# Key-value products in column groups and score products in quarters, in a float32 linear-attention and SoLU kernel

## The chip, the cores and the metric

The kernel runs on one core of a Trainium2 chip. The metric is the device time of one execution in microseconds (us). Before the change, nine runs have a median of 420.47 us and lie between 418.76 and 420.90.

TensorE multiplies matrices: a load (LDWEIGHTS) puts the stationary operand into the array, and a matmul then streams the moving operand through it. Results land in PSUM[...]. VectorE (DVE), ScalarE (ACT) and GpSimd (POOL) do the rest, each with its own queue of instructions; SyncE (SP) issues transfers.

## The reference

A recurrent attention runs over 4 batches, 8 heads, 768 tokens and a head size of 48. Its output, viewed as 3072 tokens by 384, goes through a feed-forward block with a softmax-weighted activation and a layer norm.

```python
for t in range(S):
    cur = np.einsum('bhd,bhe->bhde', u[None] * kt, vt)
    y[:, :, t] = np.einsum('bhd,bhde->bhe', rt, state + cur)
    state = w[None, :, :, None] * state + np.einsum('bhd,bhe->bhde', kt, vt)
...
h = x @ w_in
sm = e / (np.sum(e, axis=-1, keepdims=True) + 1e-09)    # e = exp(h - max)
solu = h * sm
ln = (solu - mu) / np.sqrt(var + 1e-06) * g_ln
return ln @ w_out
```

Everything is float32; w_in is 384 by 1024 and w_out is 1024 by 384.

## The kernel before

The kernel has a direct path, which runs here, and a general path behind a flag, which doesn't run. All that follows is in the direct path.

**Tiling.** The tokens are cut into 24 units of 128: six chunks (index c, C = 6) for each of four batches, with the batches innermost. A unit needs the state that the unit four places before it left, which belongs to the same batch. Heads are handled in four pairs (HP = 4, index a): the two heads of a pair (index q) lie at partitions 0 to 47 and 64 to 111 of a tile, with zeros between (P = 64 partitions for each head, of which D = 48 are used).

**Order.** The schedule is written out by hand: the loop at L829 issues the steps, and each engine takes its instructions in that order. One turn i holds, in TensorE's order:

- turn_r and turn_k of unit i + 2: transposes of r (tr_ps, L698) and of the decayed k (tk_ps, L706)
- turn_ln of unit i - 7: transposes of the activation (t_ps, L806)
- ffn_in of unit i - 2: the product with w_in (h_ps, L775), 12 records
- scores of unit i + 1: k times r per head (at, L717)
- ffn_out of unit i - 7: the product with w_out (o_ps, L817), 16 records
- finish of unit i: r times the state and scores times v (y_ps, L745), then k times v (kv_ps, L761)

Steps of units that don't exist yet, or any more, are left out. During the first turns the weights also arrive by DMA, are turned from 8-byte into float32 numbers by ScalarE, VectorE and GpSimd (L510 to L541), and column sums are taken of w_out (mean_ps, L653).

A float32 matmul appears in the trace as two records, each with a load; a transpose appears as one.

**Scores.** For each pair a and each head q, one matmul takes kT (48 rows, 128 columns) as the stationary and rT (48 rows, 128 columns) as the moving operand. The result, 128 tokens by 128 tokens, goes to the bank of q (at0 or at1, from pool psA with two buffers). Then VectorE copies it with a mask into AT (L720), only where the second token is later than the first.

**State.** After y_ps, finish computes k times v for a pair at once: kp of both heads (128 columns) is stationary, and v of both heads (96 columns) moves. Half of the result is the product of one head's k with the other head's v, and isn't wanted. The tile wt holds w^128 in the wanted blocks and zeros in the others. VectorE adds the product to the state (L764), and GpSimd multiplies the sum by wt (L765), which also sets the unwanted blocks back to zero. In the first chunk, VectorE does both at once (L767). The step is absent in the last chunk, so 20 units have it.

make_wt (L605) fills wt on GpSimd, in turn -1. The states aren't set to zero beforehand.

**Start.** VectorE first clears the pads of kpads and rpads (L482, L483), then waits for w to be turned by TensorE (wd_ps, L572), and builds the tables of powers of w (tab, pw; L573 to L583). TensorE turns one of them (kd_ps, L590), ScalarE copies it out (kdec, L591), and with kdec GpSimd decays k (kp, L675). GpSimd also makes ident, the identity for transposes, and the mask later.

**Banks.** PSUM has eight banks: two for at, two for h_ps, and four (pool psM, tag m) which tr_ps, tk_ps, t_ps, o_ps, y_ps, kv_ps and the means use in turn.

Of the kernel before, what the change touches and what calls it, by code (L numbers as in the profile page):

```python
# [9 lines left out]
F32 = mybir.dt.float32  # L10
U32 = mybir.dt.uint32
ACT = mybir.ActivationFunctionType
ALU = mybir.AluOpType
AX = mybir.AxisListType
PSUM = bass.MemoryType.PSUM
# [381 lines left out]
def direct_path(  # L397
# [26 lines left out]
    nc = tc.nc  # L424
    B, H, S, D = r.shape
    T = 128
    P = 64
    C = S // T
    HP = H // 2
    dm = H * D  # L430
# [10 lines left out]
    const = ctx.enter_context(tc.tile_pool(name="const", bufs=1))  # L441
# [1 line left out]
    fpool = ctx.enter_context(tc.tile_pool(name="fpool", bufs=2))  # L443
    wpool = ctx.enter_context(tc.tile_pool(name="wpool", bufs=2))
    small = ctx.enter_context(tc.tile_pool(name="small", bufs=4))
    psA = ctx.enter_context(tc.tile_pool(name="psA", bufs=2, space=PSUM))
    psH = ctx.enter_context(tc.tile_pool(name="psH", bufs=1, space=PSUM))
    psM = ctx.enter_context(tc.tile_pool(name="psM", bufs=4, space=PSUM))

# [12 lines left out]
    def load(i, which="krv"):  # L462
        b, c = units[i]
        for t, src, n in ((kpads, k, "k"), (rpads, r, "r"), (vts, v, "v")):
            if n in which:
                nc.sync.dma_start(out=t[i % len(t)][:, :, 0:D],
                                  in_=src[b, :, ts(c, T), :].rearrange("h s d -> s h d"))
# [12 lines left out]
                        in_=u.rearrange("h d -> (h d)").partition_broadcast(128))  # L480
    for i in range(NLD):
        nc.vector.memset(kpads[i][:, :, D:P], 0.0)  # L482
        nc.vector.memset(rpads[i][:, :, D:P], 0.0)  # L483

    def words(x):
        n, m = x.shape
        t = bass.DRamTensorHandle(x.tensor.name, (n, 2 * m), U32)
        return bass.AP(tensor=t, offset=0, ap=[[2 * m, n], [1, 2 * m]])
# [69 lines left out]
    ident = const.tile([128, 128], F32, name="ident")  # L558
# [4 lines left out]
    nc.gpsimd.memset(neg_half, -0.5)  # L563

    tab = const.tile([128, 2, HP, T], F32, name="tab")
    back, fore = tab[:, 0], tab[:, 1]
    pw = const.tile([128, 2, 8, HP], F32, name="pw")
# [27 lines left out]
    nc.gpsimd.affine_select(out=mf, in_=mf, compare_op=ALU.is_gt, fill=0.0, base=0,  # L597
                            pattern=[[1, T]], channel_multiplier=-1)
    nc.gpsimd.tensor_copy(out=later[:, 0, :], in_=mf)


    states = [const.tile([128, HP, 2, D], F32, name=f"state{b}") for b in range(B)]
    wt = const.tile([128, HP, 2, D], F32, name="wt")

    def make_wt():  # L605

        nc.gpsimd.memset(wt, 0.0)
        for q in range(2):
            rows = slice(q * P, q * P + D)
            nc.gpsimd.tensor_copy(out=wt[rows, :, q, :],  # L610
                                  in_=pw[rows, 0, 7].unsqueeze(2).to_broadcast([D, HP, D]))

    N = len(units)
    sums = const.tile([128, N], F32, name="sums")
# [53 lines left out]
    def pair(t, a):  # L668
        return t[:, 2 * a : 2 * a + 2, :].rearrange("p q d -> p (q d)")
# [9 lines left out]
    def weigh(i, engine):  # L679
        rku = live[i]["rku"] = apool.tile([128, H, D], F32, name="rku")  # L680
        engine.tensor_mul(rku, kpads[i % NLD][:, :, 0:D], u_bc)
        engine.tensor_mul(rku, rku, rpads[i % NLD][:, :, 0:D])  # L682

    def sum_own(i):
        own = live[i]["own"] = small.tile([128, H, 1], F32, name="own")
        nc.vector.tensor_reduce(out=own[:, :, 0], in_=live[i]["rku"], axis=AX.X, op=ALU.add)
# [7 lines left out]
    def turn_r(i):  # L694
        rT = live[i]["rT"] = apool.tile([128, HP, T], F32, name="rT", bufs=3)
        ps = psM.tile([128, HP, T], F32, tag="m", name="tr_ps")
        for a in range(HP):
            nc.tensor.transpose(ps[:, a, :], pair(rpads[i % NLD], a), ident)  # L698
        nc.vector.tensor_mul(rT, ps, fore)

    def turn_k(i):
        X = live[i]
        X["kT"] = apool.tile([128, HP, T], F32, name="kT")
        ps = psM.tile([128, HP, T], F32, tag="m", name="tk_ps")
        for a in range(HP):
            nc.tensor.transpose(ps[:, a, :], pair(X["kp"], a), ident)  # L706
        nc.scalar.copy(out=X["kT"], in_=ps)


    def scores(i):  # L710
        X = live[i]
        A4 = X["AT"].rearrange("p (a q) t -> p a q t", q=2)
        pss = [psA.tile([128, HP, T], F32, tag="at", name=f"at{q}") for q in range(2)]
        for a in range(HP):
            for q in range(2):
                rows = slice(q * P, q * P + D)
                nc.tensor.matmul(pss[q][:, a, :], X["kT"][rows, a, :], X["rT"][rows, a, :],  # L717
                                 start=True, stop=True)
        for q in range(2):
            nc.vector.copy_predicated(A4[:, :, q, :], later.to_broadcast([128, HP, T]), pss[q])  # L720

# [12 lines left out]
    def finish(i):  # L734
        b, c = units[i]
        X = live[i]
        vt, AT, St = vts[i % NV], X["AT"], states[b]
        vf = vt.rearrange("p h d -> p (h d)")
        y_ps = psM.tile([128, KD, 128], F32, tag="m", name="y_ps")
        last = {m: n for n, (m, h, at) in enumerate(inner)}  # L740
        opened = set()

        def into(m, lhsT, rhs, stop):
            j, g = divmod(m, 4)
            nc.tensor.matmul(y_ps[32 * g : 32 * g + 32, j, :], lhsT, rhs, start=(g not in opened),  # L745
                             stop=stop, skip_group_check=True)
            opened.add(g)

        if c > 0:
            for m in range(12):  # L750
                a, n = divmod(m, 3)
                into(m, St[:, a].rearrange("p q d -> p (q d)")[:, ts(n, 32)], X["rT"][:, a, :],
                     False)
        for n, (m, h, at) in enumerate(inner):
            into(m, vf[:, at : at + 32], AT[:, h, :], last[m] == n)
        X["xT"] = fpool.tile([128, KD, 128], F32, name="xT", bufs=LA + 1)
        nc.scalar.copy(out=X["xT"], in_=y_ps)
        if c < C - 1:
            kv_ps = psM.tile([128, HP, 2, D], F32, tag="m", name="kv_ps")
            for a in range(HP):  # L760
                nc.tensor.matmul(kv_ps[:, a], pair(X["kp"], a), vt[:, 2 * a : 2 * a + 2, 0:D],  # L761
                                 start=True, stop=True)
            if c > 0:
                nc.vector.tensor_add(St, kv_ps, St)  # L764
                nc.gpsimd.tensor_mul(St, St, wt)  # L765
            else:
                nc.vector.tensor_mul(St, kv_ps, wt)  # L767


    def ffn_in(i):  # L770
# [58 lines left out]
    for i in range(-2, N + LA + LO):  # L829
        j, l = i - LA, i - LA - LO  # L830
        if i == 0:
            nc.sync.dma_start(out=g_sb, in_=moe_g_ln.rearrange("(c p) -> p c", p=128))
        if 0 <= i and i + 4 < N:
            load(i + 4)
        if i + 2 < N:
            turn_r(i + 2)
            if i == -2:
                weigh(0, nc.vector)
            sum_own(i + 2)
            turn_k(i + 2)  # L840
        fs = [pieces[p][2] for p in now if pieces[p][2] is not None]
        for p in now:
            convert_d(p)
        now = [todo.pop(0) for _ in range(conversions.get(i, 0))]
        for n, p in enumerate(now):
            convert_a(p)
            if n == 0 or i < LA:
                convert_b(p)
            if ahead < len(pieces):
                load_weights(ahead)  # L850
                ahead += 1
        if i + 3 < N:
            decay_k(i + 3)
            if i < 0:
                weigh(i + 3, nc.gpsimd)
        for p in now[: 1 if i >= LA else 2]:
            convert_c(p)
        if 0 <= i and i + 3 < N:
            weigh(i + 3, nc.gpsimd)
        if i == -1:  # L860
            make_wt()
        if i == 10:
            check_range()
        if 0 <= l and not i > N + LA - 1:
            turn_ln(l)
        if 0 <= j < N:
            ffn_in(j)
        column_sums(fs)
        if 0 <= i + 1 < N:
            scores(i + 1)  # L870
        if 0 <= j < N:
            unit(j)
        if i + 2 < N and (i < 0 or l >= 0):
            diagonal(i + 2)
        if i >= N + LA - 1 and l + 1 < N:
            turn_ln(l + 1)
        if l == N - 1:
            check_sums()
        if 0 <= l:
            ffn_out(l)  # L880
        if 0 <= i < N:
            finish(i)
        if l < 0 <= i:
            diagonal(i + 2)
        for p in now[1:] if i >= LA else []:
            convert_b(p)
            convert_c(p)
        if KF - 1 in fs:
            column_mean()
            for f in range(KF):  # L890
                centre(f, nc.vector if f % 2 == 0 else nc.gpsimd)
# [43 lines left out]
```

## Time and profile before

| What | Value |
|---|---|
| Median of nine runs | 420.47 us (418.76 to 420.90) |
| The profiled execution | 420.26 us |
| Its span, from the first to the last instruction | 418.5 us |
| Granted TensorE clock, mean | 0.981 |
| TensorE busy with matmuls | 393.8 us (94%) |
| TensorE busy with loads (beside matmuls) | 247.3 us (59%) |
| VectorE, ScalarE, GpSimd busy | 155.6, 181.1, 147.9 us (37%, 43%, 35%) |
| at, L717: 384 records | 30.1 us busy |
| kv_ps, L761: 160 records | 23.5 us busy |
| VectorE's addition to the state, L764: 16 | 8.9 us, 558 ns each |
| GpSimd's product with wt, L765: 16 | 16.1 us, 1005 ns each |
| GpSimd's filling of wt, L607 and L610 | 0.4 and 0.9 us |

The profile is of one execution. A record of a matmul runs from its dispatch to a modelled end, so records overlap, and the time that a stage takes is read from the distance between starts, or from the chain of waits, better than from the length of records. A line of the timeline has the start, the length, the engine, the line of the kernel, the operation, the tile written and the tiles read, the shape, and how many instructions were merged into it. Its length runs from the first start to the last end.

### The profile page before, as it was taken

To read this page: it belongs to the slowest core of one execution; us is meant where nothing else is said; L and a number is where in the kernel's file an instruction comes from. 1 tells how busy PE (TensorE), PEld (TensorE's weight loads), DVE (VectorE), ACT (ScalarE), POOL (GpSimd) and SP (SyncE) were. 2 spreads that over 40 slices of the span, in tenths; PEclk is the share of its full clock that TensorE was granted. 3 is DMA by queue.
4 is the path that set the end of the run, shared out by engine and by line. 5 is a ranking of instruction groups with operands and counts; after the bars stand their busy time and mean duration, and the time that the engine had idled before them with its cause. 6 is when DMAs were issued, how large, how long until landed. Compare 5 with 4: busy or idle time off the path is not lost.

```text
span 418.5 us, 7217 instructions
## 1 busy us (share of the span) xinstructions
PE 393.8 (94%) x2873; PEld 247.3 (59%) x2873; DVE 155.6 (37%) x302; ACT 181.1 (43%) x424; POOL 147.9 (35%) x220
## 2 busy tenths in 40 slices
PE   2699899979999999999999999999999999999994
PEld 1485455655665666656656656756755655556662
DVE  5988666546224243223322422422331322022110
ACT  1875787662452552542543533523524522223210
POOL 4886666847414514414324334234130110011000
PEclk9869999999999999999999999999999999999999
DMA  8999694100403403404304214124000000000101
GB/s 172 281 198 251 138 171 76 20 2 0 77 20 58 77 2 75 77 2 75 73 3 77 59 18 77 34 42 77 20 0 20 21 1 20 20 20 19 38 19 48
DMA packets 81593, 25.93 MB, mean 62 GB/s; under 512 B 76557, under 2 KB 79758, under 8 KB 81550
## 3 DMA queue, kind: packets, MB, share of 16 engines
q1 hardware_dynamic: 81406, 25.18, 29.8%
q8 instruction: 24, 0.39, 0.4%
q10 hardware_dynamic: 144, 0.20, 0.1%
q14 instruction: 19, 0.16, 0.1%
HBM read 20.65 MB, written 4.72 MB: 61 GB/s over the span
## 4 chain that ended last, share of the span: by engine, by line
PE 84%; DVE 7%; ACT 4%; POOL 1%; issue 1%; DMA 1%; ACTq 0%; POOLq 0%; DVEq 0%
PE o_ps L817 30%; PE h_ps L775 29%; PE y_ps L745 7%; PE at L717 5%; PE t_ps L806 5%; PE kv_ps L761 3%; PE tk_ps L706 2%; DVE AT L720 2%; ACT AT L692 2%; DVE solu L787 2%; PE tr_ps L698 1%; DVE ma L524 1%; DVE ma L526 1%; DVE mag L520 1%; PE mean_ps L653 1%
## 5 line engine op out<-in xcount | busy, mean ns | idle before, releaser
L775 PE MATMUL h_ps<-w_in_sb,xT 128*128 128x512 f32 x288 | 129.0, 597 | 2.5 <-DVE solu L787 2.1
L817 PE MATMUL o_ps<-w_out_sb,lnT 128*128 128x384 f32 x384 | 129.5, 491 | 0.0
L817 PEld LDWEIGHTS o_ps<-w_out_sb,lnT 128*128 128x128 f32 x384 | 71.2, 190 | 47.5 <-issue 1.0
L775 PEld LDWEIGHTS h_ps<-w_in_sb,xT 128*128 128x128 f32 x288 | 53.3, 192 | 61.1 <-issue 59.8
L720 DVE COPY_PREDICATED AT<-later,at 128x512 f32<-128x512 uint32 x48 | 32.2, 724 | 93.2 <-ACT e L778 82.9
L778 ACT ACTIVATE e<-h_ps 128x1024 f32<-128x1024 f32 x24 | 24.5, 1022 | 91.3 <-PE h_ps L775 91.3
L692 ACT ACTIVATE AT<-ident,own 128x128 f32<-128x128 f32 x192 | 58.5, 389 | 0.0
L791 POOL TENSOR_TENSOR st<-st 128x1 f32<-128x1 f32 x24 | 4.7, 198 | 140.1 <-DVE solu L787 140.1
L789 ACT ACTIVATE e<-solu 128x1024 f32<-128x1024 f32 x24 | 25.4, 1057 | 66.5 <-DVE solu L787 66.5
L717 PEld LDWEIGHTS at<-rT,kT 48*128 48x128 f32 x384 | 25.2, 195 | 18.0 <-issue 15.0
L764 DVE TENSOR_TENSOR state<-kv_ps,state 128x384 f32<-128x384 f32 x16 | 8.9, 558 | 69.2 <-PE kv_ps L761 69.2
L675 POOL TENSOR_TENSOR kp<-kpad,kdec 128x512 f32<-128x512 f32 x24 | 31.9, 1329 | 5.3 <-ACT kdec L591 5.2
L765 POOL TENSOR_TENSOR state<-state,wt 128x384 f32<-128x384 f32 x16 | 16.1, 1005 | 47.5 <-DVE state L764 47.5
L717 PE MATMUL at<-rT,kT 48*128 48x128 f32 x384 | 30.1, 293 | 1.4 <-ACT mag L510 1.3
L787 DVE SCALAR_TENSOR_TENSOR solu<-h_ps,st,e 128x1024 f32<-128x1024 f32 x24 | 30.8, 1284 | 1.1
L808 DVE COPY lnT<-t_ps 128x512 f32<-128x512 f32 x24 | 16.4, 683 | 36.5 <-PE t_ps L806 36.5
L806 PE MATMUL t_ps<-ident,solu 128*128 128x128 f32 x192 | 25.8, 277 | 2.3 <-ACT mean_sb L661 2.1
L745 PE MATMUL y_ps<-AT,vt 128*32 128x128 f32 x768 | 26.3, 279 | 0.0
L820 ACT ACTIVATE o<-o_ps,st 128x384 f32<-128x384 f32 x24 | 13.6, 568 | 29.1 <-PE o_ps L817 14.0
L806 PEld LDWEIGHTS t_ps<-ident,solu 128*128 128x128 f32 x192 | 22.0, 142 | 5.5 <-ACT mean_sb L661 2.3
L682 POOL TENSOR_TENSOR rku<-rku,rpad 128x384 f32<-128x384 f32 x23 | 23.4, 1015 | 1.8
L761 PE MATMUL kv_ps<-vt,kp 128*128 128x96 f32 x160 | 23.5, 292 | 0.0
(80 smaller groups left out, 362.6 us busy)
## 6 DMA issues: line engine op xcount, KB each, us to landing
kpad<-in_k_dram SPq DMA_DIRECT2D x24, 192.0 KB, 4.0
rpad<-in_r_dram SPq DMA_DIRECT2D x24, 192.0 KB, 4.0
vt<-in_v_dram SPq DMA_DIRECT2D x24, 192.0 KB, 4.2
out_dram<-o SPq DMA_DIRECT2D x24, 192.0 KB, 2.1
raw<-in_moe_w_in_dram SPq DMA_DIRECT2D x6, 512.0 KB, 5.6
raw<-in_moe_w_out_dram SPq DMA_DIRECT2D x8, 384.0 KB, 3.9
u_bc<-in_u_dram ACTq DMA_DIRECT2D x1, 192.0 KB, 3.4
wq<-in_w_dram SPq DMA_DIRECT2D x1, 1.5 KB
```

The lines of the kernel that those rows point to most:

```text
L675: nc.gpsimd.tensor_mul(X["kp"].rearrange("p h d -> p (h d)"), kpads[i % NLD].rearrange("p h d -> p (h d)"), kdec.rearrange("p a d -> p (a ...
L692: nc.scalar.activation(out=AT[:, h, :], in_=ident, func=ACT.Copy, scale=X["own"][:, h])
L717: nc.tensor.matmul(pss[q][:, a, :], X["kT"][rows, a, :], X["rT"][rows, a, :], start=True, stop=True)
L720: nc.vector.copy_predicated(A4[:, :, q, :], later.to_broadcast([128, HP, T]), pss[q])
L745: nc.tensor.matmul(y_ps[32 * g : 32 * g + 32, j, :], lhsT, rhs, start=(g not in opened), stop=stop, skip_group_check=True)
L761: nc.tensor.matmul(kv_ps[:, a], pair(X["kp"], a), vt[:, 2 * a : 2 * a + 2, 0:D], start=True, stop=True)
L775: nc.tensor.matmul(h_ps[:, ts(n, NX)], X["xT"][:, j, :], w_in_sb[:, j, ts(n, NX)], start=(j == 0), stop=(j == KD - 1))
L778: nc.scalar.activation(out=e, in_=h_ps, func=ACT.Exp, accum_out=sums[:, i : i + 1])
L787: nc.vector.scalar_tensor_tensor(out=solu, in0=X["h"], scalar=rs, in1=X["e"], op0=ALU.mult, op1=ALU.mult, accum_out=tot)
L789: nc.scalar.activation(out=X["e"], in_=solu, func=ACT.Square, accum_out=ss)
L806: nc.tensor.transpose(t_ps[:, f, :], X["solu"][:, ts(4 * g + f, 128)], ident)
L817: nc.tensor.matmul(o_ps, X["lnT"][:, f, :], w_out_sb[:, f, :], start=(f == 0), stop=(f == KF - 1))
```

## The change

- **scores**: the 128 columns of kT are taken in two groups of 64 (index c). The first group multiplies all 128 columns of rT. The second multiplies only the last 64, since a later token can't lie before it. One matmul per pair and head becomes two, and the two groups write to different halves of the partitions of a bank. A quarter of each bank is never written.
- **Score banks**: at0 and at1 are made once, at the top, and VectorE sets them to zero there, ahead of the tables.
- **k times v**: one matmul per head instead of one per pair, with 64 stationary and 48 moving columns. The two heads of a pair go to partitions 0 to 63 and 64 to 127 of kv_ps, which is now 4 by 48 wide. The products of one head's k with the other's v are no longer computed.
- **State update**: two additions on VectorE and two products on GpSimd, each on 64 partitions by 4 by 48 elements, for the wanted blocks only. The factor is read from pw, repeated along the last axis.
- **wt and make_wt** are removed. ScalarE sets the four states to zero (an activation with scale 0 on a column of ident), ahead of kdec.

```diff
-    psA = ctx.enter_context(tc.tile_pool(name="psA", bufs=2, space=PSUM))
+    psA = ctx.enter_context(tc.tile_pool(name="psA", bufs=1, space=PSUM))
...
+    pss = [psA.tile([128, HP, T], F32, name=f"at{q}") for q in range(2)]
+    for ps in pss:
+        nc.vector.memset(ps, 0.0)
...
+    states = [const.tile([128, HP, 2, D], F32, name=f"state{b}") for b in range(B)]
+    for St in states:
+        nc.scalar.activation(out=St.rearrange("p a q d -> p (a q d)"),
+                             in_=ident[:, 0:1].to_broadcast([128, dm]), func=ACT.Copy, scale=0.0)
...
-    wt = const.tile([128, HP, 2, D], F32, name="wt")
-    def make_wt():
-        nc.gpsimd.memset(wt, 0.0)
-        for q in range(2):
-            rows = slice(q * P, q * P + D)
-            nc.gpsimd.tensor_copy(out=wt[rows, :, q, :],
-                                  in_=pw[rows, 0, 7].unsqueeze(2).to_broadcast([D, HP, D]))
...
     def scores(i):
...
-        pss = [psA.tile([128, HP, T], F32, tag="at", name=f"at{q}") for q in range(2)]
         for a in range(HP):
-            for q in range(2):
-                rows = slice(q * P, q * P + D)
-                nc.tensor.matmul(pss[q][:, a, :], X["kT"][rows, a, :], X["rT"][rows, a, :],
-                                 start=True, stop=True)
+            for c in range(2):
+                for q in range(2):
+                    rows = slice(q * P, q * P + D)
+                    nc.tensor.matmul(pss[q][ts(c, P), a, c * P :], X["kT"][rows, a, ts(c, P)],
+                                     X["rT"][rows, a, c * P :], start=True, stop=True)
...
-            kv_ps = psM.tile([128, HP, 2, D], F32, tag="m", name="kv_ps")
+            kv_ps = psM.tile([128, HP, D], F32, tag="m", name="kv_ps")
             for a in range(HP):
-                nc.tensor.matmul(kv_ps[:, a], pair(X["kp"], a), vt[:, 2 * a : 2 * a + 2, 0:D],
-                                 start=True, stop=True)
-            if c > 0:
-                nc.vector.tensor_add(St, kv_ps, St)
-                nc.gpsimd.tensor_mul(St, St, wt)
-            else:
-                nc.vector.tensor_mul(St, kv_ps, wt)
+                for q in range(2):
+                    nc.tensor.matmul(kv_ps[ts(q, P), a], X["kp"][:, 2 * a + q, :],
+                                     vt[:, 2 * a + q, 0:D], start=True, stop=True)
+            for q in range(2):
+                wT = pw[ts(q, P), 0, 7].unsqueeze(2).to_broadcast([P, HP, D])
+                S = St[ts(q, P), :, q]
+                if c > 0:
+                    nc.vector.tensor_add(S, kv_ps[ts(q, P)], S)
+                    nc.gpsimd.tensor_mul(S, S, wT)
+                else:
+                    nc.vector.tensor_mul(S, kv_ps[ts(q, P)], wT)
...
-        if i == -1:
-            make_wt()
```

More of the change, by code (lines that the diff above doesn't have):

```diff
@@ L599, in direct_path @@
     nc.gpsimd.tensor_copy(out=later[:, 0, :], in_=mf)
-    states = [const.tile([128, HP, 2, D], F32, name=f"state{b}") for b in range(B)]
-    wt = const.tile([128, HP, 2, D], F32, name="wt")
-    def make_wt():
-        nc.gpsimd.memset(wt, 0.0)
-        for q in range(2):
-            rows = slice(q * P, q * P + D)
-            nc.gpsimd.tensor_copy(out=wt[rows, :, q, :],
-                                  in_=pw[rows, 0, 7].unsqueeze(2).to_broadcast([D, HP, D]))
     N = len(units)
```

## The prediction

> **What bounds the kernel.** I read the mean clock and the page's busy table first (PE 94% of 418.5 us), then busy time by stretch, then the chain that ended last, then the timeline of single stretches of TensorE. By stretch (us of each engine, count of instructions, granted clock, DMA share):
>
> ```profile
> 99.00:317.00 218.00, 218.00 (x1703) 138.27 (x1701) 68.51 (x126) 92.38 (x221) 73.60 (x111) 1.00 0.24 45
> ```
>
> From 99 us TensorE never stops, at full clock, while VectorE is busy 31% and GpSimd 34% of it. The chain says the same: one unit, in order of time (start, us, what):
>
> ```profile
> 106.47 1.67 PE y_ps L745 x56
> 108.14 1.06 PE kv_ps L761 x8
> 109.20 0.44 PE tr_ps L698 x4
> 109.63 0.44 PE tk_ps L706 x4
> 110.07 0.87 PE t_ps L806 x8
> 110.94 5.15 PE h_ps L775 x12
> 116.09 1.09 PE at L717 x16
> 117.19 5.36 PE o_ps L817 x16
> ...
> 317.12 0.58 PE tr_ps L698 x4
> ```
>
> The eight pieces sum to 16.08 us and repeat with nothing of another engine between them until 371 us. The change touches two of them, kv_ps and at. The last line is from a unit without k times v (the last chunk). There tr_ps follows y_ps and takes 0.58, where after kv_ps it takes 0.44. y_ps uses column tiles of 32 and tr_ps the whole array, so **0.14 us is what a change of tile shape costs** (waiting out the matmuls in flight, then loading weights uncovered). Likewise kv_ps (1.06) contains a change from y_ps, and o_ps takes 5.36 after at, but 5.16 at 352.75 where it follows h_ps.
>
> Inside a piece I need two rates, for loading weights and for streaming. The timeline of TensorE's loads and matmuls at 251 us:
>
> ```profile
> 251.08 0.16 PEld L745 LDWEIGHTS y_ps<-rT,state 128*32 128x32 f32 x8 [0.55 <-issue]
> 251.08 0.86 PE L745 MATMUL y_ps<-rT,state 128*32 128x128 f32 x24
> 252.75 0.97 PEld L761 LDWEIGHTS kv_ps<-vt,kp 128*128 128x128 f32 x8 [0.20 <-issue]
> ```
>
> A float32 matmul leaves two records (4 kv_ps matmuls, x8). Third line: one load lasts 0.19 (page, 198 ns mean), so eight starts lie in 0.97-0.19 = 0.78, or 0.111 apart. Streaming: h_ps passes 512 columns in 5.15/12 = 0.43, which is 0.84 ns a column; 96 columns take 0.080. **So kv_ps is bound by its loads of 128 columns, not by streaming.** First line: eight loads of 32 columns, two in each of four column tiles, each lasting 0.11, have all started within 0.16-0.11 = 0.05. At the third line's rate (0.87 ns a column) eight in single file would start over 7 x 0.028 = 0.19. **So column tiles load side by side.** They also stream side by side: y_ps state starts at 251.08 and AT at 251.76, so 24 records in 0.68 = 0.028 each, where one stream of 128 columns is 0.107.
>
> **kv_ps, part by part.** Now: y_ps ends and drains (0.09), a first load (0.107), seven more at 0.112, the last stream (0.080): 0.09+0.107+0.784+0.080 = 1.06, as the chain has it. After: eight matmuls, 16 records, of 64 stationary and 48 moving columns, two column tiles at a time, so eight rounds. No row has a load of 64 columns. The bounds of a round are 0.040 (streaming 48 columns) and 0.116 (two loads of 0.058 in single file). I take half of 0.112 plus 2 ns, 0.058, because loads scale between the 32-column row (0.028 or less) and the 128-column row, and tiles load in parallel. Sum: 0.09+0.055+7 x 0.058+0.040 = 0.59. But tr_ps now follows a tiled step, so 0.44 becomes 0.58. Now 1.06+0.44 = 1.50, after 0.59+0.58 = 1.17: **0.33 us saved per unit**. The chain has 13 such units in the TensorE-bound stretch (108.14 to 301.04): 4.3 us. The seven earlier units have kv_ps beside VectorE's work: nothing.
>
> **Scores.** Now at: drain 0.09, first load 0.107, seven at 0.112, last stream 0.107: 1.09. The two q already run together as row tiles. After: sixteen matmuls, four tiles at a time, eight rounds. The tile of the first 64 tokens still streams all 128 columns in each round, so the round stays at 0.109 (what y_ps needs for 128 columns in four tiles, 4 x 0.028, less rounding); only the first load halves. 0.09+0.055+7 x 0.109+0.107 = 1.015: 0.07 saved per unit. The skipped quarter saves no stream time, since its tile only waits for the longer one. Of 24 units, 16 lie in the bound stretch: 1.2 us. Array mode changes stay as many as before at both ends of this step.
>
> **The early stretch, 45 to 90 us.** Its chain also goes through VectorE:
>
> ```profile
> 51.17 1.14 PE at L717 x16
> 52.31 1.35 DVE AT L720 x2
> ...
> 53.74 1.29 DVE solu L787 x2
> 55.03 0.48 DVE state L767
> ...
> 55.65 0.63 PE tk_ps L706 x4
> ```
>
> Here at counts (three units, 0.2 us saved), and so does the state update, since tk_ps takes kv_ps's bank. It becomes two instructions of 64 partitions by 192 elements. Nearest rows: 384 elements 0.558, a copy of 512 0.683, so 0.98 ns an element, and 192 take 0.37. Two in a row overlap by 0.10, as L720's pair does (724 ns each, 1.35 together): 0.64 for 0.558. Bounds 0 to +0.2; I take +0.08, three times: 0.25 lost. Behind it VectorE has rT, own and lnT. In the bound stretch they are covered: lnT is read by o_ps after 5.15 us of h_ps. The second t_ps, which takes kv_ps's bank there, starts about 255.03 while the addition ended at 254.48; kv_ps now ends about 0.5 earlier, so the margin grows. GpSimd's two products of 192 (384 took 1.005, so about 0.55 each) are covered, as a state is next read four units later.
>
> **Start.**
>
> ```profile
> 2.11 0.06 DVE L570 MEMSET tab<- 128x4 f32 x1
> ...
> 4.16 0.16 DVE L573 TENSOR_SCALAR pw<-wd_ps 128x4 f32<-128x4 f32 x1 [1.98 <-PE wd_ps L572]
> ...
> 8.49 0.58 ACT L591 COPY kdec<-kd_ps 128x512 f32<-128x512 f32 x1 [6.01 <-PE kd_ps L590]
> ...
> 22.57 0.90 POOL L610 COPY wt<-pw 48x192 f32<-48x192 f32 x2
> ```
>
> The two zeroings of score banks (memsets of 128 elements start 0.14 apart, so 512 take 0.14 to 0.56, and a copy of 512 takes 0.68: 0.3 to 1.4 for both, I take 1.1) fit into VectorE's 1.98 us of waiting for the DMA of w; without that cover they would cost up to 1.4. ScalarE's four zeroings (0.47 to 0.61 each, as its rows of 384) end near 5 us, ahead of kdec at 8.49; uncovered they would be 2.4. They stand behind the issue of u_bc, so no DMA moves; SP's order is unchanged. Removing wt frees 1.3 us of GpSimd at 22 us. Its next piece on the chain (L534 at 27.74) waits for VectorE, whose conversions slow down beside GpSimd (0.45 or 1.4 us for the same L524). They may shift either way: 0, bounds -1 to +1. Score banks are two before and after; at did not wait for them.
>
> **Rules weighed.** The Trainium skill, *TensorE: Matmul & The Clock Gate*, Part 3, "The mechanism", says that loads overlap matmuls in flight only when their row groups differ. kv_ps's two column tiles use the same rows, so by it each of 16 records would pay 0.055+0.040: 1.52+0.09+0.58 = 2.19 for 1.50, 9 us lost over 13 units. But by it y_ps's 56 records (0.028+0.107 each) would take 7.5 us, and the row has 1.67. I follow the row. *TensorEngine Tiling (Array Packing)*, "Key Properties": a changed tile mode drains the array. No price is given; the 0.14 above is it, 13 x 0.14 = 1.8 us, already inside my sum.
>
> **Sum.** 4.3+1.2+0.2-0.25 = 5.4 us off the profiled execution's 420.26: 414.8. The median of the runs, 420.47, is 0.2 higher, so the same gain gives **415.1**.
>
> **Rivals.**
> 1. *Loads of 64 columns hardly get shorter.* If a fixed part keeps a round at 0.085 to 0.095, kv_ps saves 0.07 to 0.14 and the whole about 2 us: 418.3. For it: no row has 64 columns. Against: the 32-column loads.
> 2. *Slower: the two column tiles load in single file.* A round is then 0.116, kv_ps 0.09+0.055+7 x 0.116+0.058+0.040 = 1.06, plus 0.58: 0.14 lost per unit, 1.8 us; scores lose 0.03, 0.5; with the state 422.9. It decides from a round of about 0.10 on. Against: the first line of loads.
> 3. *The score quarters bring nothing* (a round of 0.112, first load hidden otherwise): 416.3, within my own range.
>
> Chances: forecast, with rival 3, 0.71; rival 1 0.15; rival 2 0.09; the early conversions eating a small gain, 0.05. Range 413.6 to 418.6, from a round of 0.045 and a lucky start to rival 1. By the 0.2% (0.84 us) that a measurement can tell: faster 0.84, same 0.05, slower 0.11.
>
> **What would show it.** In the chain: kv_ps near 0.6 followed by tr_ps near 0.58, at near 1.02, a period of 15.7. kv_ps near 1.06 refutes the parallel load; tr_ps above 0.6 a dearer change of shape; at above 1.09 that four tiles hinder each other. A gap before kd_ps would mean that the zeros are not covered.

## The result and the profile after

The changed kernel takes a median of 414.57 us over ten runs (412.79 to 415.92). The kernel before takes 420.47 over 31 runs (418.56 to 422.56). The ratio is 0.9868, with a 95% interval of 0.9848 to 0.9888: 5.9 us or 1.3% faster. The forecast was 415.1.

The profiled execution took 414.53 us (span 412.8), against 420.26 (418.5). The chain that ended last shows where 5.7 us went. One unit of the stretch that TensorE bounds (start, us, what):

```profile
106.58 1.67 PE y_ps L744 x56
108.25 0.60 PE kv_ps L761 x16
108.85 0.58 PE tr_ps L696 x4
109.44 0.44 PE tk_ps L704 x4
109.87 0.87 PE t_ps L809 x8
110.75 5.15 PE h_ps L778 x12
115.90 1.02 PE at L716 x24
116.92 5.36 PE o_ps L820 x16
```

Only three pieces differ from before: kv_ps 0.60 for 1.06, tr_ps 0.58 for 0.44, and at 1.02 for 1.09. The period is 15.70 for 16.08. (The chain passes through 24 of at's 32 records, since the other 8 run beside them.) Loads and matmuls of one kv_ps step in the timeline:

```profile
123.87 0.55 PEld L761 LDWEIGHTS kv_ps<-vt,kp 128*64 128x64 f32 x16 [0.20 <-issue]
123.87 0.67 PE L761 MATMUL kv_ps<-vt,kp 128*64 128x48 f32 x16
```

A load lasts 0.138 (the mean of at's loads of the same 64 columns on the page). So the sixteen loads start within 0.55-0.14 = 0.41, which is eight rounds of two loads, 0.058 apart. Before, eight loads of 128 columns started within 0.78.

The whole difference, read from the two chains:

| Stretch | Before | After | Difference |
|---|---|---|---|
| Up to the score step near 100 us | 100.02 | 100.20 | +0.18 |
| From there to the last copy of o | 312.75 | 307.60 | -5.15 |
| From there to the end of the span | 5.73 | 5.00 | -0.73 |

The middle row is 13 x 0.31 for k times v (1.50 to 1.19, as tr_ps takes 0.59 in all but the first of these units) and 16 x 0.07 for the scores. The last row is the closing of the program, which the forecast doesn't count. It contains GpSimd's clearing of the semaphores (line, queue, operation, lengths in ns, first and last start in us). Before, then after:

```profile
L930 POOLq EVENT_SEMAPHORE_RANGE_CLEAR  x1: 135/135/135, 417.4 to 417.4; - x1
L931 POOLq EVENT_SEMAPHORE_RANGE_CLEAR  x1: 135/135/135, 412.4 to 412.4; - x1
```

From there to the end of the span it is 1.1 us before and 0.4 after. Of the experiments below, only the one that keeps wt and one matmul per pair has 1.2; the seven others have 0.4. So these 0.7 us go with the change, though by which part of it, and how, is not shown. The first row is taken apart under "Start" below.

In the early stretch, VectorE's additions now are two pieces of the chain:

```profile
63.78 1.10 PE at L716 x20
64.88 1.35 DVE AT L719 x2
...
66.31 1.29 DVE solu L790 x2
67.60 0.26 DVE state L767
...
67.89 0.37 DVE state L767
...
68.40 0.63 PE tk_ps L704 x4
```

They last 0.26+0.03+0.37 = 0.66, where L764 took 0.57. The score step became 0.04 shorter (1.14 to 1.10), so a unit takes 11.17 instead of 11.11 here.

At the start, the zeros lie in the wait for w:

```profile
2.26 1.02 DVE L486 MEMSET at<- 128x512 f32 x2
2.49 1.76 ACT L572 ACTIVATE state<-ident 128x384 f32<-128x384 f32 x4
3.29 0.06 DVE L580 MEMSET tab<- 128x4 f32 x1
...
4.21 0.16 DVE L583 TENSOR_SCALAR pw<-wd_ps 128x4 f32<-128x4 f32 x1 [0.86 <-PE wd_ps L582]
```

VectorE's wait shrank from 1.98 to 0.86, and the tables begin 0.05 later. ScalarE is done at 4.25, and kdec is at 8.54.

Run times of one version come in steps of 1.3 to 1.9 us, which the last section traces to short stretches of half clock, so below the profile decides and the time stands beside it; a version's lowest runs are compared with another's lowest.

### The profile page after: what moved, and what is told of

It is laid out like the page before. It is cut to its first block, busy times and chain, and to the rows that moved or that the text cites. A ratio compares the mean times of both kernels' runs of the same rounds, so it can differ in the third digit from the quotient of the medians.

```text
span 412.8 us, 8367 instructions
## 1 busy us (share of the span) xinstructions
PE 386.4 (94%) x3417; PEld 236.6 (57%) x3417; DVE 160.8 (39%) x324; ACT 183.1 (44%) x428; POOL 147.5 (36%) x233
## 4 chain that ended last, share of the span: by engine, by line
PE 84%; DVE 8%; ACT 4%; POOL 2%; issue 1%; POOLq 0%; ACTq 0%; DVEq 0%
PE o_ps L820 31%; PE h_ps L778 29%; PE y_ps L744 7%; PE t_ps L809 5%; PE at L716 5%; PE tk_ps L704 2%; PE tr_ps L696 2%; PE kv_ps L761 2%; DVE AT L719 2%; ACT AT L690 2%; DVE solu L790 2%; DVE ma L530 1%; DVE ma L528 1%; PE mean_ps L651 1%; ACT mag L514 1%
## 5 line engine op out<-in xcount | busy, mean ns | idle before, releaser
L767 DVE TENSOR_TENSOR state<-kv_ps,state 64x192 f32<-64x192 f32 x32 | 11.4, 355 | 63.4 <-PE kv_ps L761 62.9
L716 PEld LDWEIGHTS at<-rT,kT 48*64 48x64 f32 x768 | 22.0, 138 | 18.4 <-issue 15.0
L768 POOL TENSOR_TENSOR state<-state,pw 64x192 f32<-64x192 f32 x32 | 16.1, 503 | 39.7 <-DVE state L767 38.5
L716 PE MATMUL at<-rT,kT 48*64 48x64 f32 (+1 forms) x768 | 28.4, 263 | 1.5 <-ACT mag L514 1.3
L679 POOL TENSOR_TENSOR rku<-kpad,u_bc 128x384 f32<-128x384 f32 x23 | 23.5, 1024 | 0.0
```

The lines of the kernel that those rows point to most:

```text
L716: nc.tensor.matmul(pss[q][ts(c, P), a, c * P :], X["kT"][rows, a, ts(c, P)], X["rT"][rows, a, c * P :], start=True, stop=True)
```

## The experiments

**Each part alone.** First the change without its score matmuls (the score banks are still made once and zeroed).

```diff
         for a in range(HP):
-            for c in range(2):
-                for q in range(2):
...
-                    nc.tensor.matmul(pss[q][ts(c, P), a, c * P :], X["kT"][rows, a, ts(c, P)],
-                                     X["rT"][rows, a, c * P :], start=True, stop=True)
+            for q in range(2):
...
+                nc.tensor.matmul(pss[q][:, a, :], X["kT"][rows, a, :], X["rT"][rows, a, :],
+                                 start=True, stop=True)
```

> Theory (a kv_ps round lasts as long as the load of one 64-column tile, because column tiles load side by side): with the scores whole, kv_ps is 0.60 and the tr_ps behind it 0.58 as in the changed kernel, at is back at 1.09, and the time lies about 4.2 us below the kernel before (13 units x 0.32), near 416.2. Rival (most of the gain comes from freeing GpSimd of wt at the start, or from the scores): within 2 us of the kernel before.

Measured: 417.11 us (414.24 to 417.58, six runs) beside 419.19 for the kernel before on the same chip, ratio 0.9922 (0.9892 to 0.9952). The chain of this kernel:

```profile
125.77 0.60 PE kv_ps L760 x16
126.37 0.59 PE tr_ps L696 x4
...
133.42 1.09 PE at L715 x16
```

The stages are those that the theory named. The median gained 2.1 rather than 4.2, but the profile of this version holds two stretches of half clock past 40 us. The lowest runs of each, 414.24 and 418.54, are 4.3 apart. The rival, within 2 us of before, is excluded by the stages rather than by the median. (Removing wt is part of this version; the closing, shorter by 0.7, is in its 4.3 too, beside the 4.0 of 13 units.)

Then the scores alone, with one kv_ps matmul per pair, wt and make_wt as before.

> Theory (only the first load of a score step gets shorter, its rounds stay bound by the 128 streamed columns): at 1.02, kv_ps 1.06, tr_ps 0.44, and 1.1 us less than the kernel before (16 x 0.07), near 419.3. Rival (the skipped quarter saves its share of the stream, a quarter of 1.09): at near 0.82, and 4 us less.

Measured: 418.82 (417.47 to 420.86, twelve runs) beside 419.19, ratio 0.9975 (0.9955 to 0.9994); the lowest runs are 1.07 apart.

```profile
131.93 1.02 PE at L723 x24
132.95 5.36 PE o_ps L823 x16
138.31 1.67 PE y_ps L751 x56
139.97 1.06 PE kv_ps L767 x8
141.03 0.44 PE tr_ps L703 x4
```

at is 1.02, not 0.82: skipping a quarter of the products doesn't save a quarter of the time. By lowest runs the parts gain 4.3 and 1.1, together 5.4 of the whole's 5.8 (412.79 against 418.56).

**Is the quarter worth anything?** The second group multiplies all 128 columns of rT:

```diff
-                    nc.tensor.matmul(pss[q][ts(c, P), a, c * P :], X["kT"][rows, a, ts(c, P)],
-                                     X["rT"][rows, a, c * P :], start=True, stop=True)
+                    nc.tensor.matmul(pss[q][ts(c, P), a, :], X["kT"][rows, a, ts(c, P)],
+                                     X["rT"][rows, a, :], start=True, stop=True)
```

> The changed kernel, but the second group of 64 tokens multiplies all 128 columns, so no quarter is skipped. Theory (the round waits for the longer tile): at stays at 1.02 and the time stays that of the changed kernel within 0.5 us. Rival (the shorter tile's end frees something): at rises to 1.1 or more, and 1.3 us or more are lost.

Measured: 414.86 (413.17 to 416.08). The chain has `1.03 PE at`, now through all 32 records:

```profile
130.23 1.03 PE at L716 x32
131.26 5.36 PE o_ps L820 x16
```

One hundredth of a microsecond per step is all that the skipped quarter brings. The longer tile sets the end, and the score part gains by its shorter first load (about 0.05) and by rounds of 0.109 where loads of 128 columns took 0.112 (0.02). The single records of a step of the changed kernel (at 116 us) show that the shorter tile doesn't wait for its partner, as the forecast put it: it runs ahead, and its last matmul starts 0.21 before the last of the longer tile.

**Side by side by right, or by neighbourhood?** The same matmuls of k times v, the second column tile's after the first's:

```diff
-            for a in range(HP):
-                for q in range(2):
+            for q in range(2):
+                for a in range(HP):
```

> The changed kernel, but kv_ps takes the four matmuls of the first column tile one after the other, then the four of the second. Theory A (each tile works through its own matmuls, whatever stands between them in the program): kv_ps stays near 0.60, no change in time. Theory B (side by side only with a neighbour in the program): sixteen rounds of 0.058 instead of eight, kv_ps near 1.06, 0.46 x 13 = 6 us lost, all of the gain.

Measured: 416.60 (416.30 to 417.90). kv_ps takes 0.87, between the two theories. Counting its loads by stretch (bounds and length in us, busy with loads, their number in brackets, clock, DMA share and GB/s):

```profile
122.46:122.74 0.28, 0.27 (x5) 1.00 0.20 59
122.74:122.95 0.21, 0.21 (x9) 1.00 0.00 0
122.95:123.20 0.25, 0.25 (x8) 1.00 0.00 0
```

A load that spans a border counts in both stretches. By the single records of the trace, five loads begin in the first 0.28 us, 0.055 to 0.059 apart as the loads of one tile are. In the second stretch two such series run together, and in the third one is alone. So the second tile began 0.27 after the first, ahead of three loads of the first tile that stand before it in the program, and kv_ps is 0.27 longer. TensorE does reach past matmuls that wait for a busy tile, but here only over those three. Neither theory as I put it was right. In the changed kernel neighbours alternate, so this doesn't show there. It costs 13 x 0.27 = 3.5 us, more than half of the gain, and the lowest runs differ by as much (416.30 and 412.79).

**The price of the shape.** Four column tiles of 32, as y_ps has them:

```diff
-                for q in range(2):
-                    nc.tensor.matmul(kv_ps[ts(q, P), a], X["kp"][:, 2 * a + q, :],
+                for g in range(4):
+                    q, half = divmod(g, 2)
+                    nc.tensor.matmul(kv_ps[ts(g, 32), a], X["kp"][:, 2 * a + q, ts(half, 32)],
                                      vt[:, 2 * a + q, 0:D], start=True, stop=True)
```

> The changed kernel, but k times v takes four column tiles of 32 (each head's k in two halves), the tile shape of y_ps. Theory (a round lasts as long as the longer of one tile's load and its stream, and a change of tile shape costs what it cost in the rows of the kernel before): no change of shape between y_ps and kv_ps, loads of 0.028 hide behind streams of 0.040, eight rounds of 0.04 to 0.05, kv_ps 0.32 to 0.40 instead of 0.60, tr_ps stays at 0.58; 13 x 0.2 to 0.28 = 2.6 to 3.6 us below the changed kernel. Rival (double the instructions cost more than the load saves; a round has a floor near 0.058): kv_ps 0.5 or more, less than 1.3 us gained.

Measured: 412.72 (411.12 to 414.32), ratio to before 0.9806 (0.9777 to 0.9835).

```profile
125.11 1.67 PE y_ps L744 x56
126.77 0.34 PE kv_ps L762 x32
127.11 0.59 PE tr_ps L696 x4
```

kv_ps falls from 0.60 to 0.34. That is 0.043 for each of eight rounds, near the 0.040 in which 48 columns stream and above the 0.028 of a load of 32, so a round is now bound by streaming, and the change of shape after y_ps is gone. The gain is 13 x 0.26 = 3.4 us by stage, as forecast, but only 1.9 by medians. Past 40 us this profile has more half clock than any other (bounds and length in us, TensorE busy and count, granted clock, DMA share and GB/s):

```profile
44.40:51.22 6.82, 6.18 (x8) 0.50 0.57 126
95.60:99.01 3.41, 2.97 (x7) 0.50 0.00 0
```

The changed kernel's profile has 3.4 us of it, a third of this. That probably hides the rest of the gain, but no two runs with the same count could be compared.

**How much cover the zeros have.** The two zeroings of score banks three times over (`for ps in pss * 3`).

> The changed kernel with the two score banks set to zero three times over. Theory (VectorE's wait for the transfer of w covers the zeros: 0.86 us of it are left in the changed kernel, and one zeroing occupies 0.51): four more take 2.0 us, 1.2 us past the cover, so the transposes of kd_ps start near 8.6 instead of 7.39. Rival (the zeros are hidden wherever they stand, the start is bound by transfers): kd_ps stays within 0.2 of 7.39.

One execution, 417.11 us. The start of kd_ps in the changed kernel, then VectorE's zeros and kd_ps here:

```profile
7.39 0.71 PEld L600 LDWEIGHTS kd_ps<-ident,tab 128*128 128x128 f32 x4 [3.30 <-DVE tab L593]
```

```profile
2.26 3.19 DVE L486 MEMSET at<- 128x512 f32 x6
...
8.55 0.71 PEld L600 LDWEIGHTS kd_ps<-ident,tab 128*128 128x128 f32 x4 [4.23 <-DVE tab L593]
```

kd_ps starts at 8.55 instead of 7.39: of 2.17 more on VectorE, 1.16 came through. The cover is real, and short: it took up 1.0 us, near the 0.86 of waiting that the changed kernel has left.

**One change of shape fewer.** The score step goes behind ffn_out, next to y_ps, and unit's VectorE work comes ahead of the score copies:

```diff
         column_sums(fs)
-        if 0 <= i + 1 < N:
-            scores(i + 1)
         if 0 <= j < N:
             unit(j)
...
         if 0 <= l:
             ffn_out(l)
+        if 0 <= i + 1 < N:
+            scores(i + 1)
         if 0 <= i < N:
             finish(i)
```

> The changed kernel with the score step behind ffn_out instead of ahead of it, and unit's VectorE work ahead of the score copies. Theory (each change of tile shape costs time, and this order has one change fewer per turn): o_ps falls from 5.36 to 5.16 in the 16 units of the bound stretch, 3.2 us; in the early stretch VectorE's chain no longer stands between score copies and h_ps, 0 to 3 us more; so 3 to 6 us below the changed kernel. Rival (the drain is paid at the next step anyhow): y_ps or at grow by the same 0.2 and nothing is gained in the bound stretch.

Measured: 406.89 (406.45 to 408.43), ratio to before 0.9688 (0.9661 to 0.9716), 7.7 us below the changed kernel and more than I expected.

```profile
94.80 5.40 PE o_ps L820 x16
...
214.22 5.15 PE h_ps L778 x12
219.37 5.16 PE o_ps L820 x16
224.53 1.02 PE at L716 x24
225.55 1.67 PE y_ps L744 x56
227.22 0.60 PE kv_ps L761 x16
```

o_ps is 5.16, at and y_ps are unchanged: 0.20 less per turn, so the drain isn't paid elsewhere. Of the 16 turns 14 show this; the first o_ps, behind a wait, takes 5.40, and one takes 5.43. From the first y_ps after an o_ps to the last copy of o, the bound stretch is 2.6 us shorter. In the early stretch a turn now lasts 10.28 (h_ps at 65.97 and 76.25) instead of 11.17, and that y_ps starts at 94.80+5.40+1.02 = 101.22 instead of 106.58. Of these 5.4 us, 1.7 are a stretch of half clock that only the changed kernel's profile has (last section). So the order gains 3.7 in the early stretch and 2.6 in the bound one, together 6.3, which is also the distance of the lowest runs (412.79 and 406.45). The early stretch gave more than the 3 us that I had allowed.

**Both together.**

> Tiles of 32 for k times v and the late score step together. Theory (both act on TensorE alone and at different places): their gains add, 6 to 9 us below the changed kernel. Rival (TensorE is no longer the bound once it is this short, VectorE or ScalarE take over): less than two thirds of the sum.

Measured: 405.23 (403.32 to 405.93), ratio to before 0.9626 (0.9596 to 0.9657).

```profile
120.08 0.34 PE kv_ps L762 x32
...
127.47 5.16 PE o_ps L821 x16
```

Both stages are as in the two alone. The median is 9.3 below the changed kernel, where the two alone gave 1.9 and 7.7; the lowest runs are 9.5 apart, beside 3.4 by stage and 6.3. The gains add, and this is the fastest version: 15.2 us below the kernel before.

## Why the prediction was right

- **kv_ps.** I took 0.058 for a round of loads that no row showed, and 0.59 for the step; they are 0.058 and 0.60, and the first experiment shows that this part alone brings it. That column tiles load side by side came from one line, eight short loads begun within 0.05. Rival 2 (single file) would have made kv_ps 1.06. It does turn up, in part, when neighbours don't alternate (0.87).
- **The rule on loads.** By the Trainium skill, *TensorE: Matmul & The Clock Gate*, Part 3, "The mechanism", where loads overlap matmuls in flight only if the row groups differ, kv_ps and tr_ps should have become 2.19 together. They take 1.18 to 1.19, with two tiles on the same rows. Here the measurement decides against the rule. The same section also lets a load be pulled ahead of matmuls in flight when it targets the background weight buffer, which the forecast left out. And o_ps before, with one tile on all rows, already departs from the bare rule: 16 records in 5.16 us are 0.32 each, as long as 384 columns stream (0.84 ns each), with no time left for loads.
- **The change of shape.** tr_ps grew to 0.58, the value read from the chunk without kv_ps. The tile of 32 and the late score step show the same price from the other side.
- **Scores.** 1.015 forecast, 1.02 measured. That the quarter itself saves nothing is shown by the full second group. Rival 3, no gain at all, fails at the stage: each step is 0.07 shorter.
- **Early stretch.** I had 0.2 us gained by at and 0.25 lost by the additions, 0.05 lost in all. The chain lost 0.24: its three units (mean_ps from 50.38 to 83.65 before, from 51.85 to 85.36 after) take 33.51 instead of 33.27. at gave 0.04 per unit instead of 0.07, and the additions cost 0.16 in the first unit and 0.09 in the second. Both terms are small, and both were mis-sized.
- **Start.** The two zeroings took 1.02 (1.1 forecast), and ScalarE's four took 1.76 (up to 2.4). All were covered. The chain reached h_ps at 44.77 instead of 44.99; whether GpSimd, freed of wt, brought these 0.2 is not shown. That the chain is 0.18 later near 100 us comes from the 0.24 above and from the clock: the stretch of half clock cost 1.7 here and 1.5 (in t_ps and h_ps, behind 92 us) before.
- **The sum.** The mechanism was right, and the stretch bound by TensorE gave 5.15 of the 5.5 forecast for it. That the totals agree so well (5.7 in the profiles, 5.9 by medians, 5.4 forecast) is in part luck: the closing of the program, which no term of the forecast holds, became 0.73 shorter and made up for the rest.

## What to carry to other kernels

Ask of a small matmul whether its load or its stream is longer. If it is the load, splitting the stationary operand into column tiles shortens it, since tiles load and stream side by side, as long as neighbours in the program go to different tiles. Work that is skipped inside one tile of a round saves nothing while another tile takes longer. Each change of tile shape on a saturated TensorE costs about 0.14 to 0.2 us here, so order the steps such that equal shapes stand together. The late score step, which did that and also changed VectorE's order, gained 6.3 us, about as much as the tiling, but at most 2.8 of them (14 turns of 0.2) from the shapes.

## What the hardware did that I had not expected

**The look-ahead between tiles is short.** With eight loads of one tile ahead of it in the program, the other tile began only when five of them had started (0.27 us), though alternating tiles start within 0.01 of each other.

**Half-clock stretches.** Both kernels have some 10 us of half clock in the start, up to about 28 us. Past 40 us the profiles before and after each have one more stretch of it, at different places (bounds and length in us, TensorE busy and count, granted clock, DMA share and GB/s). Before:

```profile
45.00:48.00 3.00, 3.00 (x7) 1.00 0.14 20
92.40:95.40 3.00, 2.67 (x7) 0.50 0.00 0
```

After:

```profile
45.00:48.00 3.00, 3.00 (x4) 0.50 0.13 23
92.40:95.40 3.00, 1.00 (x6) 1.00 0.00 0
```

The h_ps caught in it takes 7.08 where it takes 5.39 at the same place before, 1.7 us more:

```profile
44.77 7.08 PE h_ps L778 x12
44.99 5.39 PE h_ps L775 x12
```

The profiles of the experiments have none, one or two of these stretches past 40 us, without a change of code that would explain it. Such a stretch lasts 3.4 us (in the experiment with tiles of 32, one lasts 6.8). In each profile that has them, TensorE mostly waits in the 3.4 us before: it is busy for 0.98 to 1.50 of them. Such a wait doesn't always bring one: the kernel before is busy for 1.33 of the 3.4 us up to 45.0 and goes on at full clock.

Run times of one kernel lie in steps of about that size (412.8, 414.5 and 415.9 for the changed kernel), and the three profiles without such a stretch (the full second group, the heads in turn, the late score step) are of runs on the lowest step of their kernel. So a part that is worth 1 us is better read from its stage than from a few medians. Whether the late score step avoids these stretches, as five of its six runs within 0.6 us suggest, is left open.
